# Applying the modulation of chunk 5 of batch 0 on ScalarE ahead of the normalization of token tile 2, in a diffusion-transformer block

## The chip, the cores and the metric

The kernel runs on one core of one Trainium2 chip. The metric is the device time of one execution in microseconds (us). All executions quoted are fast, at a granted TensorE clock of 0.996 to 1.000.

## The reference

A block of a diffusion transformer: `c` is turned into six modulation vectors per batch; then attention and an MLP, each behind a layer norm that is scaled and shifted by them.

```python
B, N, D = x.shape              # 2, 256, 1152;  F = 4 * D
mod = (_silu(c) @ w_mod).reshape(B, 6, 1, D)
shift_a, scale_a, gate_a, shift_m, scale_m, gate_m = [mod[:, i] for i in range(6)]
h = _layernorm(x) * (1 + scale_a) + shift_a
# ... attention over h, two heads -> a (projected by wo)
x = x + gate_a * a
h2 = _layernorm(x) * (1 + scale_m) + shift_m
m = _gelu(h2 @ w_fc1) @ w_fc2
return x + gate_m * m
```

The change lies between the projection by `wo` and the product with `w_fc1`.

## The kernel before

The 512 tokens are four tiles of 128: tiles 0 and 1 are batch 0, tiles 2 and 3 are batch 1. The 1152 features are nine chunks of 128 (numbered 0 to 8). For each tile the projection is accumulated, added to the residual `x1`, normalized over the features and turned round by a transposing DMA into `hT`, which has features on partitions. Then "modulation" multiplies each chunk of `hT` by its scale and adds its shift, one instruction per chunk and batch, on VectorE ("d") or ScalarE ("a"):

```python
def ln2_modulate(b, k, eng="d"):
    h = hT[:, k, b * N:(b + 1) * N]
    if eng == "a":
        return nc.scalar.activation(
            h, h, ACT.Identity, bias=shift_m[:, k, b:b + 1], scale=scale_m[:, k, b:b + 1],
        )
    return nc.vector.tensor_scalar(
        h, h, scale_m[:, k, b:b + 1], shift_m[:, k, b:b + 1], op0=ALU.mult, op1=ALU.add,
    )

def ln2_normalize(t, split, between):
    rstd = small.tile([P, 1], FP32, name="rstd", tag="rstd")
    nc.scalar.activation(rstd[:], mv2[:, t, 1:2], ACT.Sqrt, bias=eps_t[:], scale=1.0)
    for k, eng in between:
        ln2_modulate(0, k, eng)
    # ... VectorE: reciprocal, nb = -mean * rstd; xn2 allocated
    cs = 5 * P if split else D
    # ... if split, VectorE normalizes columns cs to D
    nc.scalar.activation(xn2[:, 0:cs], x1[:, t, 0:cs], ACT.Identity, bias=nb[:], scale=rstd[:])
    nc.scalar.dma_start_transpose(hT[:, :, t * P:(t + 1) * P], xn2[:])
```

`BETWEEN` says which chunks of batch 0 are modulated between the square root and the normalization of a tile. The loop runs over tiles and thirds of the features. The rest of batch 0's chunks is modulated beside the last third of tile 3:

```python
BETWEEN = {2: ((0, "d"), (1, "d"), (2, "a"), (3, "a")), 3: ((8, "d"),)}

def ln2_stats(t, i):
    nc.vector.bn_stats(stats2[t][:, i, :], x1[:, t, i * PW:(i + 1) * PW])
    if i == NPD - 1:
        nc.vector.bn_aggr(mv2[:, t, :], stats2[t][:].rearrange("p a b -> p (a b)"))
        ln2_normalize(t, t % 2 == 1, BETWEEN.get(t, ()))

for o, (t, i) in enumerate(order):
    last = o == len(order) - 1
    if last:
        ln2_modulate(0, 4)
    wo_group(t, i, i < NPD - 1)          # the projection: nine products a group
    if o:
        ln2_stats(*order[o - 1])
    if last:
        ln2_modulate(0, 5, "a")
        ln2_modulate(0, 7, "a")
        ln2_modulate(0, 6)
ln2_stats(*order[-1])
```

Then comes fc1. For batch 0 its first six output blocks are computed chunk by chunk ("stepped"), so that the TensorE can begin as soon as chunk 0 is modulated: six 128x256 products for chunk 0, six for chunk 1, and so on. Each engine executes its own instructions in the order in which the program issues them.

```python
for b in range(B):
    for stepped in (True, False):
        ms = range(0, MSPLIT // 2) if stepped else range(MSPLIT // 2, MSPLIT)
        # ...
        steps = [(m, k) for k in range(KD) for m in ms] if stepped else [(m, k) for m in ms for k in range(KD)]
        # ... one product of w_f1 and hT[:, k, batch b] for each (m, k)
    if b == 0:
        mods = [ln2_modulate(1, k) for k in range(KD)]
```

## Time and profile before

| | before |
|---|---|
| device time, median of 4 runs | 245.31 us (245.11 to 245.61) |
| span of the profiled execution | 244.1 us |
| TensorE busy | 237.0 us, 97% |
| TensorE waits from 80 us on | one, 0.36 us, on ScalarE's modulation |

First, lines from the page of the profile of the kernel before: the span; busy time (share) and instruction count of each engine; the granted clock of the TensorE in tenths in 40 slices; the shares of the chain of work that ended last; its costliest group (busy us, mean ns of one; idle before and its releaser). PE is the TensorE, PEld its weight loads, DVE VectorE, ACT ScalarE.

```profile
span 244.1 us, 3930 instructions
...
PE 237.0 (97%) x1679; PEld 142.6 (58%) x1679; DVE 91.7 (38%) x198; ACT 62.1 (25%) x122; POOL 25.4 (10%) x37
...
PEclk9999999999999999999999999999999999999999
...
PE 89%; DVE 4%; DMA 2%; ACT 2%; ACTq 1%; issue 1%; DVEq 0%
...
L682 PE MATMUL pacc<-hT,w_f 128*128 128x256 bf16 (+1 forms) x432 | 70.7, 326 | 0.4 <-ACT hT L600 0.4
```

The TensorE is busy nearly always. The fc1 products (L682) have one idle time, 0.4 us, released by "ACT hT L600", a modulation on ScalarE. The view of the TensorE's waits from 80 us to the end (line that waited, on what; us in total, times, longest) shows that this is the only wait after the start-up:

```profile
PE pacc L682 <- ACT hT L600: 0.4, 1, 0.4
```

The timeline of ScalarE around it (start in us from the span's start, duration in us, engine, line, operation, what it writes and reads, how many in a row; in brackets the idle time before and its releaser; ACTq is ScalarE's sequencer, here issuing a transposing DMA):

```profile
97.94 0.29 ACT L609 ACTIVATE rstd<-mv,eps_t 128x1 f32<-128x1 f32 x1 [3.12 <-DMA hT<-xn]
98.14 1.08 ACT L600 ACTIVATE hT<-hT,shift_m,scale_m 128x256 bf16<-128x256 bf16 x2
99.17 1.35 ACT L622 ACTIVATE xn<-x,nb,rstd 128x1152 bf16<-128x1152 f32 x1
100.55 1.30 ACTq L623 DMA_TRANSPOSE hT<-xn  x1
101.90 1.09 ACT L600 ACTIVATE hT<-hT,shift_m,scale_m 128x256 bf16<-128x256 bf16 x2 [1.38 <-issue]
103.17 0.29 ACT L609 ACTIVATE rstd<-mv,eps_t 128x1 f32<-128x1 f32 x1 [0.18 <-DVE mv L648]
```

Line by line: square root of tile 2; chunks 2 and 3; normalization of tile 2; the issue of its transpose, which holds ScalarE up for 1.30 us; only then chunks 5 and 7; then tile 3's square root. Chunk 5, the first of the pair at 101.90, is ready at 102.50.

The TensorE's timeline over the same time and up to the small product for the second gate, `pg`:

```profile
98.76 3.44 PE L682 MATMUL pacc<-hT,w_f 128*128 128x256 bf16 x30
102.55 65.14 PE L682 MATMUL pacc<-hT,w_f 128*128 128x256 bf16 x393 [0.36 <-ACT hT L600]
167.62 0.33 PE L442 MATMUL pg<-fold,folded 128*36 128x32 f32 x4
```

Thirty products are chunks 0 to 4 at six each. Then the TensorE waits for chunk 5, and from 102.55 it goes on without a gap. The timeline of the weight loads shows the same place in a second way:

```profile
81.19 17.34 PEld L632 LDWEIGHTS <-big 128*128 128x128 bf16 x108 [0.20 <-issue]
98.60 3.43 PEld L682 LDWEIGHTS <-w_f 128*128 128x128 bf16 x31
102.55 64.65 PEld L682 LDWEIGHTS <-w_f 128*128 128x128 bf16 x392 [0.53 <-issue]
```

One load normally follows another after about 0.11 us. The 31st load (chunk 5's first) runs ahead of its product and ends at about 102.02; then there is an idle time of 0.53 us.

Batch 1 is modulated by VectorE as soon as the transpose of tile 3 has landed. Its timeline line for that shows when, and for how long VectorE waited:

```profile
110.04 2.40 DVE L603 TENSOR_SCALAR hT<-hT,scale_m,shift_m 128x256 bf16<-128x256 bf16 x9 [5.68 <-DMA hT<-xn]
```

I use one more measure below, the **stretch**: from the first weight load of the projection (81.19, L632 above) to the `pg` product (167.62). It holds everything that the change touches. Here it is 167.62 - 81.19 = 86.43 us. What follows it, from `pg` to the end of the span, takes 76.43 to 76.46 us in all eleven profiles of this study, so a gain or loss in the stretch is passed on whole. Stretches are differences of times printed to 0.01 us and can be off by that much.

### The profile page before, as it was taken

To read this page: it belongs to the slowest core of one execution; us is meant where nothing else is said; L and a number is where in the kernel's file an instruction comes from. 1 tells how busy PE (TensorE), PEld (TensorE's weight loads), DVE (VectorE), ACT (ScalarE), POOL (GpSimd) and SP (SyncE) were. 2 spreads that over 40 slices of the span, in tenths; PEclk is the share of its full clock that TensorE was granted. 3 is DMA by queue.
4 is the path that set the end of the run, shared out by engine and by line. 5 is a ranking of instruction groups with operands and counts; after the bars stand their busy time and mean duration, and the time that the engine had idled before them with its cause. 6 is when DMAs were issued, how large, how long until landed. Compare 5 with 4: busy or idle time off the path is not lost.

```text
span 244.1 us, 3930 instructions
## 1 busy us (share of the span) xinstructions
PE 237.0 (97%) x1679; PEld 142.6 (58%) x1679; DVE 91.7 (38%) x198; ACT 62.1 (25%) x122; POOL 25.4 (10%) x37
## 2 busy tenths in 40 slices
PE   6999999999999999999999999999999999999993
PEld 2585444456667665788854444444665656565673
DVE  2761562126414589913006999910000000000001
ACT  6632251145122521671422233322000000000000
POOL 1000000031000233200000000001222111111111
PEclk9999999999999999999999999999999999999999
DMA  6999999999996999227999994799300000010000
GB/s 227 327 333 360 371 326 390 391 390 393 342 374 93 385 392 182 48 51 249 393 392 374 326 327 121 221 327 320 102 16 16 19 16 16 17 33 19 16 19 16
DMA packets 47308, 53.28 MB, mean 218 GB/s; under 512 B 8371, under 2 KB 34107, under 8 KB 47291
## 3 DMA queue, kind: packets, MB, share of 16 engines
q1 hardware_dynamic: 39840, 50.14, 61.0%
q10 hardware_dynamic: 6939, 1.71, 5.1%
q0 software_dynamic: 512, 1.19, 1.4%
q8 instruction: 13, 0.21, 0.4%
q14 instruction: 4, 0.03, 0.0%
HBM read 50.14 MB, written 1.19 MB: 210 GB/s over the span
## 4 chain that ended last, share of the span: by engine, by line
PE 89%; DVE 4%; DMA 2%; ACT 2%; ACTq 1%; issue 1%; DVEq 0%
PE pacc L738 29%; PE pacc L682 28%; PE pacc L543 7%; PE pacc L472 7%; PE pk L263 4%; PE pk L292 2%; PE pwarm L156 2%; PE pacc L632 2%; PE pa L577 2%; PE ps_s L501 2%; PE pn L375 1%; DMA hT<-xn 1%; DVE stats L646 1%; DMA c_sb<-in_c_dram 1%; DVE tmp L637 1%; ACT xn L622 1%
## 5 line engine op out<-in xcount | busy, mean ns | idle before, releaser
L682 PE MATMUL pacc<-hT,w_f 128*128 128x256 bf16 (+1 forms) x432 | 70.7, 326 | 0.4 <-ACT hT L600 0.4
L738 PE MATMUL pacc<-w_f,gT 128*128 128x384 bf16 (+2 forms) x468 | 70.5, 314 | 0.0
L738 PEld LDWEIGHTS <-gT 128*128 128x128 bf16 x468 | 44.4, 98 | 26.2
L682 PEld LDWEIGHTS <-w_f 128*128 128x128 bf16 x432 | 42.2, 98 | 28.2 <-issue 0.5
L744 DVE TENSOR_TENSOR tmp<-pacc,gate 128x384 f32<-128x384 f32 (+2 forms) x13 | 6.8, 526 | 65.6 <-PE pacc L738 57.8
L714 ACT ACTIVATE gT<-pacc 128x512 bf16<-128x512 f32 x24 | 14.3, 597 | 32.7 <-PE pacc L682 32.7
L424 DVE SCALAR_TENSOR_TENSOR part<-w_gate_m,s,part 128x1152 f32<-128x1152 bf16 x16 | 21.3, 1413 | 0.0
L543 PE MATMUL pacc<-w_v,hT 128*128 128x384 bf16 x108 | 17.9, 326 | 0.0
L472 PE MATMUL pacc<-hT,w_q 128*128 128x512 bf16 x81 | 17.8, 379 | 0.0
L632 PE MATMUL pacc<-w_o,big 128*128 128x384 bf16 x108 | 17.7, 326 | 0.0
L746 POOL TENSOR_TENSOR o_sb<-tmp,x 128x384 bf16<-128x384 f32 (+1 forms) x12 | 11.6, 970 | 54.4 <-DVE tmp L744 54.4
L632 PEld LDWEIGHTS <-big 128*128 128x128 bf16 x108 | 10.5, 98 | 7.0 <-issue 0.2
L543 PEld LDWEIGHTS <-hT 128*128 128x128 bf16 x108 | 10.4, 98 | 7.2 <-issue 0.4
L263 PE MATMUL pk<-big,w_k 128*128 128x256 bf16 (+2 forms) x90 | 13.4, 294 | 0.4 <-ACT big L250 0.4
L472 PEld LDWEIGHTS <-w_q 128*128 128x128 bf16 x81 | 7.8, 98 | 9.9 <-DMA w_q<-in_wqkv_dram 0.5
L638 POOL TENSOR_TENSOR x<-tmp,x_sb 128x384 f32<-128x384 f32 x8 | 7.3, 912 | 35.3 <-DVE tmp L637 35.3
L263 PEld LDWEIGHTS <-w_k 128*128 128x128 bf16 x90 | 7.5, 98 | 3.4 <-issue 0.4
L156 PE MATMUL pwarm<-zeros 128*128 128x512 bf16 x19 | 8.0, 580 | 1.2 <-DVE eps_t L93 1.2
L703 ACT ACTIVATE gT<-pacc 128x512 bf16<-128x512 f32 x12 | 6.5, 598 | 9.5 <-PE pacc L682 9.5
L422 DVE TENSOR_SCALAR part<-w_gate_m,s 128x1152 f32<-128x1152 bf16 x2 | 1.6, 818 | 17.6 <-DMA w_gate_m<-in_w_mod_dram 17.6
L446 POOL DMA_DIRECT2D gates_dram<-nat_v x2 | 1.1, 531 | 68.0 <-DVE nat_v L444 68.0
L637 DVE TENSOR_TENSOR tmp<-pacc,gate 128x384 f32<-128x384 f32 x12 | 6.6, 547 | 2.7 <-PE pacc L632 2.7
(93 smaller groups left out, 156.4 us busy)
## 6 DMA issues: line engine op xcount, KB each, us to landing
w_f<-in_w_fc_dram SPq DMA_DIRECT2D x14, 864.0 KB, 10.2
w_f<-in_w_fc_dram SPq DMA_DIRECT2D x2, 2592.0 KB, 15.5
w_f<-in_w_fc_dram SPq DMA_DIRECT2D x2, 1728.0 KB, 10.5
w_shift_a<-in_w_mod_dram SPq DMA_DIRECT2D x3, 864.0 KB, 11.4
w_q<-in_wqkv_dram SPq DMA_DIRECT2D x3, 864.0 KB, 12.0
w_gate_a<-in_w_mod_dram SPq DMA_DIRECT2D x3, 864.0 KB, 10.0
w_v<-in_wqkv_dram SPq DMA_DIRECT2D x3, 864.0 KB, 13.3
w_shift_m<-in_w_mod_dram SPq DMA_DIRECT2D x3, 864.0 KB, 15.2
```

Of the source, the lines that this page charges most:

```text
L156: nc.tensor.matmul(dst[:], zeros[:, 0:P], zeros[:], start=True, stop=True)
L263: nc.tensor.matmul(pk[m][:, c0:c1], w_k[:, k, m * P:(m + 1) * P], hT0[:, k, c0:c1], start=(k == 0 and c0 == 0), stop=(k == KD - 1), skip_g ...
L424: nc.vector.scalar_tensor_tensor(part[:, b, :], wg[:, k, :], s32[:, k, b:b + 1], part[:, b, :], op0=ALU.mult, op1=ALU.add,)
L472: nc.tensor.matmul(pacc[:], w_q[:, k, m * P:(m + 1) * P], hT[:, k, :], start=(k == 0), stop=(k == KD - 1),)
L543: nc.tensor.matmul(pacc[:], hT[:, k, t * P:(t + 1) * P], w_v[:, k, pnl * PW:(pnl + 1) * PW], start=(k == 0), stop=(k == KD - 1),)
L632: nc.tensor.matmul(pacc[:], aT[:, k, t * P:(t + 1) * P], w_o[:, k, c0:c1], start=(k == 0), stop=(k == KD - 1),)
L637: nc.vector.tensor_tensor(tmp[:], pacc[:], gate_a[:, b, c0:c1], op=ALU.mult)
L638: (nc.gpsimd if pool_add else nc.vector).tensor_tensor(x1[:, t, c0:c1], tmp[:], x_sb[:, t, c0:c1], op=ALU.add)
L682: nc.tensor.matmul(dst, w_f1[m // KD][:, k, ml * P:(ml + 1) * P], hT[:, k, c0:c1], start=start, stop=(k == KD - 1), **kw,)
L714: nc.scalar.activation(gT[:, m, :], pacc[:], ACT.Gelu_apprx_tanh)
L738: nc.tensor.matmul(pacc[:], gT[:, kk, t * P:(t + 1) * P], w_f2[j][:, r, c0 - n * PW:c0 - n * PW + cw], start=(kk == 0), stop=(kk == KF - 1),)
L746: (nc.vector if last else nc.gpsimd).tensor_tensor(o_sb[:], tmp[:], x1[:, t, c0:c0 + cw], op=ALU.add)
```

## The change

The intent is to have chunk 5 ready before the TensorE asks for it, by moving one ScalarE instruction ahead of the longer normalization and the transpose issue. The whole diff:

```diff
-    BETWEEN = {2: ((0, "d"), (1, "d"), (2, "a"), (3, "a")), 3: ((8, "d"),)}
+    BETWEEN = {2: ((0, "d"), (1, "d"), (2, "a"), (3, "a"), (5, "a")), 3: ((8, "d"),)}
@@
         if last:
-            ln2_modulate(0, 5, "a")
             ln2_modulate(0, 7, "a")
             ln2_modulate(0, 6)
```

## The prediction

> **What bounds the kernel now.** The TensorE. The page of the profile shows it busy 97% of the 244.1 us span at a granted clock of 1.000. The chain of waits runs through it: "PE pacc L682 65.14 us x393" from 102.55 us, 2 us more of it, then "PE pacc L738 70.30 us x468" to 240.30. From 102.55 us on the view of waits shows no wait of the TensorE: whatever starts this block earlier moves the end by as much, and nothing else does.
>
> From 80 us on, the view of waits names one wait of the TensorE: 0.36 us at L682 on "ACT hT L600". The timeline shows it. The first fc1 product visits nine chunks in order, six 128x256 products a chunk; thirty (chunks 0 to 4) run from 98.76 to 102.20 us; the next needs chunk 5. ScalarE does: sqrt of tile 2 (97.94), chunks 2 and 3 (98.14 to 99.22), normalization of tile 2 (99.17 to 100.52), issue of its transpose (100.55 to 101.85), and only then chunks 5 and 7 (101.90 to 102.99). Chunk 5 is ready at about 102.5; TensorE restarts at 102.55.
>
> **What the change does.** No work is added or removed: one 128x256 ScalarE instruction moves ahead of the tile-2 normalization. One takes 588 ns, a pair 1.08 us, so a further one costs about 0.49 us. The Trainium skill (ScalarE: Activation LUTs, "What ACT_TABLE_LOAD costs") gives 186 ns + 93 ns per pointer operand + 0.833 ns per element, here 585 ns, and an overlap of 93 ns; the trace agrees.
>
> Estimated ScalarE order after: chunks 2, 3, 5 from 98.14 to 99.7; normalization to 101.0; transpose issue 101.04 to 102.34; chunk 7 to 102.98; sqrt of tile 3 at 103.17 as before, because it waits for VectorE's aggregate (103.14).
>
> **On the critical path.** Chunk 5 is ready 2.5 us before it is needed, so the 0.36 us wait goes. No new wait should appear: at 0.115 us a product, chunk 6 is needed at 102.89 (ready 102.39), chunk 7 at 103.58 (102.98), chunk 8 at 104.27 (103.33). The tile-2 transpose lands 0.5 us later, at 104.2, but batch 1 waits for the tile-3 transpose, which landed at 109.95. Batch 1's first chunk is ready at 110.38 and is now needed at about 111.05 instead of 111.4; VectorE then takes 0.27 us a chunk, TensorE 0.69. The tail depends on TensorE alone: the weights of fc2 land by 171.7 us, and the gate's chain starts from a TensorE product.
>
> **Prediction.** 245.45 - 0.36 = 245.1 us, with 244.6 to 245.6 to hold it 8 times in 10 (the runs before spread over 0.45 us). Faster by over 2%: 0.005; within 2%: 0.99; slower by over 2%: 0.005. The gain, 0.15%, is small against the spread, but should be real in the trace.
>
> **What would show each step.** Right: three L600 instructions back to back from 98.14 us, one left after the transpose issue; no L682 wait on L600; one run of about 426 L682 products from 98.76; every later TensorE time about 0.35 us earlier; span about 243.7 us; tile 3's sqrt near 103.17. Wrong: a new TensorE wait on chunk 7 near 103.6, or on VectorE L603 near 111.
>
> **What would make it wrong.** The tile-3 landing is fragile: 15 of 16 completions came by 108.35 us and one at 109.95, behind a 16 KB instruction transfer at 107.9. If that falls worse, batch 1's slack of 0.65 us is used up and the gain given back. Or a semaphore wait covers chunk 5 by counting a later ScalarE instruction. Or the spread between runs hides 0.36 us.

## The result, and the profile after

| | before | after |
|---|---|---|
| device time, median of 4 runs | 245.31 us (245.11 to 245.61) | 244.69 us (244.62 to 244.81) |
| span of the profiled execution | 244.1 us | 242.8 us |
| TensorE waits from 80 us on | 0.36 us | none |
| first weight load of the projection | 81.19 us | 80.44 us |
| stretch | 86.43 us | 85.92 us |

The ratio of the times is 0.9974, with a 95% interval of 0.9960 to 0.9988. A ratio here is the mean time of one kernel's fast runs over that of the other's fast runs of the same rounds, so it is not quite the ratio of the quoted medians. The interval lies wholly below 1, so the small gain is real.

The same lines of the page after (lines past the change have numbers lower by one):

```profile
span 242.8 us, 3919 instructions
...
PE 235.0 (97%) x1668; PEld 142.3 (59%) x1679; DVE 91.7 (38%) x198; ACT 62.1 (26%) x122; POOL 25.4 (10%) x37
...
PEclk9999999999999999999999999999999999999999
...
PE 93%; DMA 3%; DVE 1%; issue 0%; SPq 0%; ACT 0%; DVEq 0%
...
L681 PE MATMUL pacc<-hT,w_f 128*128 128x256 bf16 (+1 forms) x427 | 70.3, 325 | 0.3
```

The 0.4 us at the first fc product is gone. (The 0.3 us shown in its place are holes of single missing records: there are 427 products of 432 in this trace, while the weight loads, of which none is missing, show no gap.) All waits of the TensorE after, the start-up included:

```profile
PE pwarm L156 <- DVE eps_t L93: 1.2, 1, 1.2
PE pc L159 <- DMA c_sb<-in_c_dram: 1.1, 1, 1.1
PE pm L231 <- DMA w_scale_a<-in_w_mod_dram: 0.5, 1, 0.5
PE pk L263 <- ACT big L250: 0.4, 1, 0.4
PE pt L241 <- DVE xn L218: 0.3, 1, 0.3
```

No wait on ScalarE's hT is left. One that the first profile of the kernel before didn't have is at the start, "pm" on the weights, 90 us ahead of the change; it is taken up below. ScalarE's timeline after:

```profile
97.19 0.29 ACT L609 ACTIVATE rstd<-mv,eps_t 128x1 f32<-128x1 f32 x1 [3.12 <-DMA hT<-xn]
97.40 1.58 ACT L600 ACTIVATE hT<-hT,shift_m,scale_m 128x256 bf16<-128x256 bf16 x3
98.89 1.33 ACT L622 ACTIVATE xn<-x,nb,rstd 128x1152 bf16<-128x1152 f32 x1
100.25 1.31 ACTq L623 DMA_TRANSPOSE hT<-xn  x1
101.61 0.60 ACT L600 ACTIVATE hT<-hT,shift_m,scale_m 128x256 bf16<-128x256 bf16 x1 [1.38 <-issue]
102.43 0.29 ACT L609 ACTIVATE rstd<-mv,eps_t 128x1 f32<-128x1 f32 x1 [0.22 <-DVE mv L648]
```

This is the order that was intended: three modulations in a row, and one left behind the transpose issue. Tile 3's square root still comes straight after VectorE's aggregate. The TensorE and its weight loads after:

```profile
98.01 68.42 PE L681 MATMUL pacc<-hT,w_f 128*128 128x256 bf16 x418
166.36 0.33 PE L442 MATMUL pg<-fold,folded 128*36 128x32 f32 x4
```

```profile
80.44 17.34 PEld L632 LDWEIGHTS <-big 128*128 128x128 bf16 x108 [0.20 <-issue]
97.85 68.08 PEld L681 LDWEIGHTS <-w_f 128*128 128x128 bf16 x423
```

One run of 423 loads where there were 31 and 392 with a hole between. The stretch is 166.36 - 80.44 = 85.92 us, 0.51 us less than before. The span fell by 1.3 us, but 0.75 us of that (81.19 - 80.44) is there before the projection begins, ahead of anything that the change touches. So two questions stay open from the two traces alone: why 0.51 us for a wait of 0.36, and whether the 0.75 us belong to the change. Batch 1's line after, for the slack there:

```profile
108.84 2.40 DVE L603 TENSOR_SCALAR hT<-hT,scale_m,shift_m 128x256 bf16<-128x256 bf16 x9 [5.22 <-DMA hT<-xn]
```

The first chunk of batch 1 is written at about 109.2 us; the first weight load of batch 1 is at 109.69, its product about 0.1 us later: no wait, as before.

### The profile page after: what moved, and what is told of

Same layout as the page of the kernel before. It is cut to its first block, busy times and chain, and to the rows that moved or that the text cites. A ratio compares the mean times of both kernels' runs of the same rounds, so it can differ in the third digit from the quotient of the medians.

```text
span 242.8 us, 3919 instructions
## 1 busy us (share of the span) xinstructions
PE 235.0 (97%) x1668; PEld 142.3 (59%) x1679; DVE 91.7 (38%) x198; ACT 62.1 (26%) x122; POOL 25.4 (10%) x37
## 4 chain that ended last, share of the span: by engine, by line
PE 93%; DMA 3%; DVE 1%; issue 0%; SPq 0%; ACT 0%; DVEq 0%
PE pacc L737 29%; PE pacc L681 29%; PE pacc L543 7%; PE pacc L632 7%; PE pacc L472 7%; PE pk L263 4%; DMA w_scale_a<-in_w_mod_dram 3%; PE pk L292 2%; PE pa L577 2%; PE ps_s L501 2%; PE pn L375 1%; DVE stats L173 1%; PE pm L231 1%; PE pt L241 1%; PE pg L453 0%
## 5 line engine op out<-in xcount | busy, mean ns | idle before, releaser
L156 PE MATMUL pwarm<-zeros 128*128 128x512 bf16 x18 | 6.4, 512 | 1.2 <-DVE eps_t L93 1.2
```

## The experiments

Theory A: the gain is the wait on chunk 5 and nothing else; a wait of the TensorE costs the distance between the weight loads around it less the usual 0.11 us, which is about 0.16 us more than the idle time shown for the products; the rest of the difference between the two profiles is chance in the start-up. Rivals: A2, the shown idle time is the whole cost; B, the change shortens the start as well; C, what helps is moving any instruction ahead of the normalization. All results were correct. Each kernel was timed in five runs beside nine of the kernel before.

### null_before: the kernel before again

No edit.

> The kernel before, unchanged, as one more kernel. The two profiles so far differ by 1.3 us in span, of which about 0.75 us is already there at the first attention-output product (81.19 against 80.45 us), ahead of anything the change touches. Theory A (the gain is the wait on chunk 5; the rest of the profiles' difference is chance in the start-up): ratio 1.000 within 0.001, the wait on ACT hT again at 0.36 us, first L682 to the gate product again about 68.9 us, but the first attention-output product may begin anywhere from 80.4 to 81.2 us. Rival B (the change itself shortens the start, by its different instruction streams): the start repeats 81.2 us within 0.1.

Measured: 245.15 us (245.04 to 245.51), ratio 0.9996 (0.9983 to 1.001). The wait was again 0.36 us, the idle time of the weight loads again 0.53, the stretch 86.44 us. But the projection began at 80.37 us, not at 81.19. So the start-up of one and the same kernel moves by 0.8 us between executions, and rival B falls. Over all eleven profiles the projection began between 80.37 and 81.26 us, though all but one of these kernels have the same instructions up to there. With chunk 5 moved it was 80.44 to 80.94 us, without that 80.37 to 81.26: no shift shows.

A part of that can be seen. The start of the TensorE in the first profile of the kernel before, then in that of the changed kernel (14 warm-up products at L156, then the first real one at L231):

```profile
3.35 5.95 PE L156 MATMUL pwarm<-zeros 128*128 128x512 bf16 x14
9.13 0.59 PE L231 MATMUL pm<-sT,w_scale_a 128*128 128x2 bf16 x18
```

```profile
3.41 4.81 PE L156 MATMUL pwarm<-zeros 128*128 128x512 bf16 x14
8.70 0.60 PE L231 MATMUL pm<-sT,w_scale_a 128*128 128x2 bf16 x18 [0.48 <-DMA w_scale_a<-in_w_mod_dram]
```

In the first the warm-ups took 5.95 us and ran past the landing of the weights; in the second the TensorE sped up sooner and waited for the weights. The Trainium skill (TensorE: Matmul & The Clock Gate, "What's actually happening") says that the clock rises after a free-running window of activity of about 3.4 us, so that the number of slow products varies from run to run. The traces agree: the warm-ups (128x512) came every 0.43 us up to the last, at 8.87 us, in the one, and until about 6.4 us in the other, where they came every 0.22 us afterwards. The clock records in the trace files begin their stretch at full clock at 8.96 and at 6.72 us, 5.6 and 3.3 us after these warm-ups began. (The views count the time before the first record as full clock, so PEclk doesn't show it.) In the eleven profiles this stretch lasts 235.52 us or 238.93 us, which are 3.41 us apart and 69 and 70 times 3.413, so it fits a window of that length. That accounts for 0.43 of the 0.75 us (9.13 against 8.70). Most of the rest is a wait of the first weight load of the q projection for its data, 0.53 against 0.21 us in the two traces.

### again_after: the changed kernel again

No edit.

> The changed kernel again. Theory A: ratio to before 0.9980 (0.5 us faster), no wait of the TensorE on ACT hT, first fc1 product to gate product about 68.35 us (0.5 us less than before), whatever the start-up does. Theory A2 (the idle time shown for the TensorE is the whole cost): 0.36 us, so ratio 0.9985, block 68.5 us. Rival B: the attention-output products again begin near 80.45 us, and the ratio is 0.9975 or lower.

Measured: 244.95 us (244.81 to 245.02), ratio 0.9982 (0.9970 to 0.9995). No wait on hT; the projection began at 80.84 us; the stretch is 166.76 - 80.84 = 85.92 us, the same as in the first profile of this kernel. So the stretch repeats to 0.01 us where the span doesn't, and the gain in it is 0.51 us.

### seven_ahead: chunk 7 moved in place of chunk 5

```diff
-    BETWEEN = {2: (..., (2, "a"), (3, "a")), 3: ((8, "d"),)}
+    BETWEEN = {2: (..., (2, "a"), (3, "a"), (7, "a")), 3: ((8, "d"),)}
@@
             ln2_modulate(0, 5, "a")
-            ln2_modulate(0, 7, "a")
```

> Chunk 7 instead of chunk 5 goes ahead of the tile-2 normalization, so ScalarE does the same reordering and the normalization moves by the same 0.5 us, but chunk 5 comes even later, by one slot. Theory A: the wait on chunk 5 grows from 0.36 to about 0.85 us, the distance between the weight loads around it from 0.63 to about 1.1 us, and the kernel is 0.5 us slower than before (ratio 1.002). Rival C (what helps is moving work ahead of the normalization, whichever chunk): as fast as after, ratio 0.998.

Measured: 245.63 us (245.40 to 246.26), ratio 1.0014 (1.0002 to 1.0027). The TensorE's timeline, then that of its weight loads:

```profile
98.08 3.44 PE L681 MATMUL pacc<-hT,w_f 128*128 128x256 bf16 x30
102.32 65.14 PE L681 MATMUL pacc<-hT,w_f 128*128 128x256 bf16 x393 [0.80 <-ACT hT L600]
```

```profile
102.32 64.64 PEld L681 LDWEIGHTS <-w_f 128*128 128x128 bf16 x392 [0.97 <-issue]
```

The stretch is 86.87 us, 0.95 over the changed kernel and 0.44 over the kernel before. The same reordering with the wrong chunk makes the kernel slower by nearly what the right one gains: rival C falls. The loads' idle time, 0.97 us, gives the loss; the products' shown 0.80 us does not.

### five_on_vector: chunk 5 late, on VectorE

```diff
-            ln2_modulate(0, 5, "a")
+            ln2_modulate(0, 5)
```

> Chunk 5 stays late, but on VectorE just ahead of chunk 6, ready about 102.4 us instead of 102.5. Theory A: the wait shrinks to about 0.24 us and changes its name to DVE hT, weight-load distance about 0.5, gain 0.12 us (ratio 0.9995, hardly visible in the times, visible in the trace). Tile 3's chain on VectorE starts about 0.27 us later, with no effect. Rival C: no gain or a loss, as nothing was moved ahead.

Measured: 245.14 us (245.02 to 245.62), ratio 0.9994 (0.9982 to 1.0007), so nothing can be said from the times. The two timelines:

```profile
101.85 65.14 PE L682 MATMUL pacc<-hT,w_f 128*128 128x256 bf16 x393 [0.26 <-DVE hT L603]
```

```profile
101.85 64.65 PEld L682 LDWEIGHTS <-w_f 128*128 128x128 bf16 x392 [0.43 <-issue]
```

The wait has shrunk to 0.26 us and its releaser is now VectorE's modulation. The stretch is 86.34 us, 0.42 over the changed kernel; the loads' idle time is 0.43.

### five_and_seven_ahead: both chunks ahead of the normalization

```diff
-    BETWEEN = {2: (..., (2, "a"), (3, "a"), (5, "a")), 3: ((8, "d"),)}
+    BETWEEN = {2: (..., (2, "a"), (3, "a"), (5, "a"), (7, "a")), 3: ((8, "d"),)}
@@
-            ln2_modulate(0, 7, "a")
```

> The change, and chunk 7 goes ahead of the tile-2 normalization as well. Theory A (only a wait of the TensorE counts): nothing more is gained, because chunk 7 already came 0.6 us before it was needed; no wait on hT, stretch from the first attention-output product to the gate product 85.9 us as in the changed kernel (86.43 in the kernel before), ratio 0.998. Rival C (each instruction moved ahead of the normalization gains about 0.5 us): 85.4 us, ratio 0.996.

Measured: 244.75 us (244.70 to 244.90), ratio 0.9981 (0.9969 to 0.9994), stretch 85.92 us. Nothing is gained over the changed kernel, because no product waited for chunk 7. Moving the normalization of tile 2 by another half microsecond cost nothing either.

### split_tile2: chunk 5 behind a shorter normalization

This one separates theory A from A2. Chunk 5 stays where it was in the kernel before, but is ready just when the products of chunk 4 are shown to end.

```diff
-        cs = 5 * P if split else D
+        cs = 6 * P if t == 2 else 5 * P if split else D
```

with VectorE taking the columns from `cs` on, as the kernel already does for tiles 1 and 3:

```diff
         if cs < D:
             nc.vector.tensor_scalar(xn2[:, cs:D], ...)   # unchanged, now also for tile 2
```

> The kernel before, with chunk 5 left behind the tile-2 normalization, but that normalization made shorter on ScalarE: 768 of its 1152 columns, VectorE takes the other 384. Chunk 5 should then be ready about 0.32 us earlier than before, at a point where the shown idle time of the TensorE is nearly gone. Theory A (a wait costs the distance between the weight loads around it, less the usual 0.11 us; the shown idle time is 0.16 us short of that): shown wait 0.00 to 0.06 us, distance 0.27 to 0.34 us, stretch from the first attention-output product to the gate product 86.05 to 86.15 us, so 0.15 to 0.2 us still lost against the changed kernel (85.91). Theory A2 (the shown idle time is the whole cost): shown wait 0.00 to 0.06 us and stretch 85.91 to 85.97 us. In the times either is 0.1 to 0.2% faster than before.

Measured: 245.06 us (244.89 to 245.60), ratio 0.9992 (0.9978 to 1.0005). ScalarE's timeline (the normalization, now 128x768; the transpose issue; chunks 5 and 7), the TensorE's, and that of the weight loads:

```profile
99.24 1.03 ACT L622 ACTIVATE xn<-x,nb,rstd 128x768 bf16<-128x768 f32 x1
100.30 1.30 ACTq L623 DMA_TRANSPOSE hT<-xn  x1
101.65 1.09 ACT L600 ACTIVATE hT<-hT,shift_m,scale_m 128x256 bf16<-128x256 bf16 x2 [1.38 <-DVE tmp L637]
```

```profile
98.82 68.62 PE L682 MATMUL pacc<-hT,w_f 128*128 128x256 bf16 x418
```

```profile
102.30 64.64 PEld L682 LDWEIGHTS <-w_f 128*128 128x128 bf16 x392 [0.21 <-issue]
```

The timeline of the products is one unbroken run, and the view of waits has no wait of the TensorE there. (By the single records one product starts at 101.987 us and is shown to end at 102.260, and the next starts at 102.300: a hole of 0.04 us, too small for the views to list.) The weight loads have a hole of 0.21 us at chunk 5, the only one among the loads of fc1 up to the one at `pg`, which every kernel has. The stretch is 86.11 us, 0.19 over the changed kernel. So a wait of which the products show next to nothing cost 0.2 us, and A2 falls.

### late_tile3_3 and late_tile3_6: tile 3 held up on ScalarE

These test the prediction's account of what lies next behind the gain: batch 1 waits for tile 3's transpose. In the changed kernel, n idle copies ahead of tile 3's square root:

```diff
+    spare = const.tile([P, T], BF16, name="spare")
@@ def ln2_normalize(t, split, between):
+        if t == NT - 1:
+            for _ in range(n):                       # 3 or 6
+                nc.scalar.copy(spare[:], zeros[:])
```

> The changed kernel with three idle 128x512 ScalarE copies ahead of tile 3's square root, which comes about 1.4 us later; the TensorE's slack at batch 1's first chunk was about 0.5 us in the changed kernel's trace (chunk written at 109.14, first product of batch 1 at 109.69). If the landing of tile 3's transpose moves by as much as its issue: wait on DVE hT near 110 us, 0.9 us lost, stretch 86.8 us, slower than the kernel before (ratio 1.002). If the landing is set by the instruction transfer that it collides with (106.3 to 107.2 us there), a later issue goes clear of it, lands about 109.0 us, and nothing or at most 0.3 us is lost: stretch 85.9 to 86.2 us.

Measured with three: 244.84 us (244.66 to 245.52), ratio 0.9989 (0.9975 to 1.0002), stretch 85.91 us, no wait. The transpose was issued at 106.18 us instead of 104.61 in again_after, but its last completion came at 109.39 instead of 109.19.

> Six copies, tile 3's square root about 3.0 us later. Landing at 110.4 us if it goes clear of the instruction transfer, 111.7 if it moves by as much: a wait on DVE hT either way, 1.1 or 2.5 us lost, stretch 87.0 or 88.4 us, ratio about 1.003 or 1.008. No wait at all would mean that batch 1 doesn't hang on this landing, and the prediction's account of the slack is wrong.

Measured with six: 246.48 us (246.29 to 246.68), ratio 1.0048 (1.0034 to 1.0062), stretch 87.66 us, 1.74 over the changed kernel. The transpose was issued at 107.99 and had landed at 111.20 us. Neither expected number came, though the transpose took 3.2 us as in the case without a collision: six copies made its issue 3.4 us later than in again_after (107.99 against 104.61), not 3.0. The TensorE's timeline and that of the weight loads:

```profile
111.71 56.81 PE L685 MATMUL pacc<-hT,w_f 128*128 128x256 bf16 x315 [1.40 <-DVE hT L603]
```

```profile
111.70 0.44 PEld L685 LDWEIGHTS <-w_f 128*128 128x128 bf16 x5 [1.68 <-DVE hT L603]
112.33 55.69 PEld L685 LDWEIGHTS <-w_f 128*128 128x128 bf16 x310 [0.19 <-issue]
```

After 108 products, the end of batch 0, the TensorE now waits for VectorE's modulation of batch 1. The products' shown 1.40 us is again short of the loss: with the 0.16 us of theory A it is 1.56, and a second small hole, 0.19 us at the loads and not shown at the products, brings it to 1.74 (1.56 + 0.19 - 0.01, the last being the usual idle time between loads). The loads' own 1.68 us at the first wait is too much by about 0.1 here, because the first load of batch 1 waited as well instead of running ahead of its product as at chunk 5.

Why did 1.57 us of delay (106.18 - 104.61) cost only 0.20 us at the landing in the first of the two? From the start of the issue to the last completion the transpose takes 3.2 us (109.39 - 106.18, and 111.20 - 107.99) in these two, but 4.6 us in again_after and 5.0 in the kernel before. In the two slower cases a 16,384-byte packet of the queue of kind "instruction" was on one of the DMA engines while the transpose's packets ran or just as they ended: 106.70 to 107.64 us in again_after, 107.94 to 108.89 in the kernel before, where 15 of 16 completions were in at 108.35 and the last at 109.95. In the two quicker cases the packet was over before the transpose's first packet. It is not every overlap that delays: in seven_ahead such a packet began 0.2 us before the transpose's last one (106.82 against 107.03 us), and the transpose still landed 3.2 us after its issue. The Trainium skill (Runtime: NRT & Kernel Launch, "Instruction fetch mechanics") says that instructions are fetched in blocks of 16 KiB by a DMA queue and that the cost of a block boundary is "mostly hidden"; that this packet is such a fetch is my reading of its size and queue. The traces agree on the size, and a transpose of tile 3 during whose packets such a packet ran took 1.2 to 1.8 us longer here (4.4 to 5.0 us, eight profiles) in all cases but seven_ahead. It was not tested by moving the fetch alone, so its being the cause is argued from these timings, not shown. There is a rival: the transpose of tile 0, issued near 90 us while 0.74 to 0.80 MB of weights were loaded, took 4.9 to 5.3 us in all eleven profiles. In two of them (seven_ahead and five_on_vector) a packet of this kind was over before its first packet. So such a packet is not the only thing that makes a transpose slow.

### warm12_after: two warm-up products fewer

```diff
-    warm(14, pwarm)
+    warm(12, pwarm)
```

> The changed kernel with 12 warm-up products instead of 14. In six profiles so far the first real product began at 8.57 to 9.13 us, at its weights' landing (about 8.6) in some and only after the last of 14 warm-ups in the others, by how soon the TensorE went from 0.43 to 0.21 us a warm-up. Theory D (the 14 warm-ups overrun the landing in some executions, and that is the spread of 0.5 us between runs of one kernel): the first real product always begins at 8.6 to 8.7, mean gain about 0.2 us over the changed kernel (ratio to before about 0.997), and a smaller spread. Rival E: fewer warm-ups leave the TensorE slow for longer, and it is the same or slower than the changed kernel.

Measured: 244.73 us (244.58 to 244.88), ratio 0.9979 (0.9967 to 0.9992), stretch 85.92 us. In its profile the warm-ups stayed slow throughout, and still the first real product waited 0.25 us for its weights, and began at 8.81 us. Against the changed kernel (0.9982 in one set of rounds, 0.9974 in another) no gain can be told: inconclusive. It is no worse, and rival E isn't supported.

## Why the prediction was right

The main points against the runs:

| predicted | shown |
|---|---|
| 245.1 us, range 244.6 to 245.6 | 244.69 and, in other rounds, 244.95 us: inside |
| the wait on chunk 5 goes, no new wait | so in all four profiles with chunk 5 moved and tile 3 not held up |
| the gain is 0.36 us | the gain in the stretch is 0.51 us: mis-sized |
| tile 3's square root unchanged | unchanged, straight after VectorE's aggregate |
| slack of 0.5 us at chunk 6 | about 0.3 us (written at 101.66, first product at 101.94), the least of the chunks modulated late |
| slack of 0.6 us at chunk 7 | about 0.4 us (written at 102.21; first weight load for it at 102.49, product about 0.1 later): a product takes 0.109 us in the stream, not the 0.115 reckoned with |
| slack of 0.65 us at batch 1 | 0.38 to 0.64 us in the four profiles with chunk 5 moved and tile 3 not held up, but by luck, see below; three copies on ScalarE fitted, six didn't |

The mechanism held: one instruction was late, the TensorE waited for it, and everything after that hangs on the TensorE alone. Seven_ahead shows that it is this chunk and not the reordering; five_and_seven_ahead shows that an earlier time for a chunk that nobody waits for is worth nothing. The time alone would prove little: the range of 1.0 us is about twice the gain, and the kernel before, at 245.31 and 245.15 us, lies in it too. What confirms the prediction are the traces and the experiments.

The slack at batch 1 came out near the forecast by luck. With 0.115 us a product the prediction put batch 1's first product at 111.05 us after the change, on the time scale of the profile before; but there it begins at 111.06 us already without the change, and its chunk is ready at 110.39. The change takes 0.52 us off, which would have left only about 0.15 us. More was left because tile 3's transpose took 4.5 to 4.8 us from issue to landing in the four profiles, and not 5.0 us as before.

The term that was mis-sized is "the 0.36 us wait goes" in the sum 245.45 - 0.36. I took the idle time shown for the TensorE as the cost of the wait. A 128x256 product is shown for 0.273 us, but in a full stream the next starts after 0.109 us (the start times of successive products in the trace). The shown end of the last product before a wait therefore lies 0.164 us past the moment at which the next could have started, and the idle time is counted only from there. 0.36 + 0.16 = 0.52 us, which is what the stretch lost. The Trainium skill has both numbers (TensorE: Matmul & The Clock Gate, "Single matmul latency" and "Back-to-back issue gap"): (398 + N) / 2.4 = 272.5 ns and N / 2.4 + 2.5 = 109.2 ns for N = 256, and the trace agrees with both. The second section calls its formula the gap of isolated products and gives other figures for a stream in which each product has its weight load, about 131 ns at N = 512; here such a stream kept to the formula, with 109 ns at N = 256 and 216 ns at N = 512 (the later fc1 products). It also says (Perfetto Trace Analysis, "Tensor Engine Instruction (MATMUL, LD_WEIGHTS)") that the end of a TensorE record is estimated. I could have known. Four sizes of the wait show the rule at this product size; all differences are to the 85.92 us of the changed kernel:

| kernel | idle of products | idle of weight loads | stretch | over the changed kernel |
|---|---|---|---|---|
| seven_ahead | 0.80 | 0.97 | 86.87 | 0.95 |
| before, null_before | 0.36 | 0.53 | 86.43, 86.44 | 0.51, 0.52 |
| five_on_vector | 0.26 | 0.43 | 86.34 | 0.42 |
| split_tile2 | 0.04, not listed | 0.21 | 86.11 | 0.19 |
| after, again_after, five_and_seven_ahead | none | none | 85.92 | 0 |

The products' idle time is short of the loss by about 0.16 us in each row that has a wait. The loads' idle time gives it to 0.02 us in all of them. By the single records the stretch is 86.432 and 86.434 us in before and null_before and 85.914 or 85.915 us in the last row, so the gain is 0.52 us. The distance between the product starts around each wait (1.068, 0.630, 0.532 and 0.313 us), less 0.109, gives the four losses to 0.005 us. Late_tile3_6, the fifth size, fits with 0.16 us added to the products' idle time, as shown there, but not by the loads' alone.

The first pair of medians differs by 0.62 us, more than 0.51. The intervals of both sets of rounds with the changed kernel (0.29 to 0.98 us, and 0.12 to 0.74 us, worked out from the ratios at 245.4 us) hold 0.51, so nothing more needs explaining. The 1.3 us between the first two spans are 0.51 us of the change and 0.75 us of the start-up; the two add up to the 1.26 us by which `pg` came earlier (167.62 - 166.36).

What stays open: what sets the 0.8 us of spread in the start beyond the warm-up and the q weights, and whether the delay of tile 3's transpose is really the instruction packet's.

## What to carry to other kernels

Where one engine runs without a gap, look for its single waits, find the one instruction that each wait ends with, and move that instruction alone; here moving its neighbour as well gained nothing, and moving the neighbour in its place lost 0.44 us. Price such a wait not by the idle time between product records, whose ends overlap the next start, but by the distance between the starts of the products around it less the usual distance (where loads run ahead, the hole in the weight loads is the same): at 128x256 here, a wait of up to 0.16 us leaves no idle time between the product records at all. And judge a half-microsecond change from a stretch of the trace that starts after the start-up's chance and ends where the effect has settled, with the same kernel run twice beside it.

## What the Trainium skill lacked or had wrong

- Perfetto Trace Analysis, and TensorE: Matmul & The Clock Gate: neither says that idle time shown between products understates a wait by latency less issue gap. In these runs 0.36 us shown cost 0.51, and 0.04 that the views don't list cost 0.19, at 128x256; the idle time of the weight loads (0.53 and 0.21 us) was right to 0.02.
- Runtime: NRT & Kernel Launch: the cost of an instruction block's boundary is called mostly hidden. It was hidden here from the TensorE, but tile 3's transposing DMA took 4.4 to 5.0 us from issue to last completion in eight of the nine profiles in which a 16,384-byte instruction packet ran during its packets, against 3.2 us where none did (read from timings, not tested alone).
- DMA: Bandwidth & Descriptors: it has transfer rates for transposing DMAs, but no time from issue to landing for one of this size. A 128x1152 bf16 transpose within SBUF took 3.2 us from the start of its issue to landing when undisturbed (tiles 1 and 2 in all profiles), and its issue held up ScalarE for about 1.30 us. That hold and the normalization ahead of it (1.35 us) are what made chunk 5 late.
